# Block-sparse attention into a SwiGLU layer: the same 1,550 operations in a newly searched order

## The chip, the cores and the metric

The kernel runs on one core of a Trainium2 chip. The metric is the device time of one execution in microseconds (us). The core has five engines, each with an instruction stream of its own that it works through strictly in order: TensorE (PE in the profile, its weight loads PEld), VectorE (DVE), ScalarE (ACT), GpSimd (POOL) and SyncE (SP), which here only issues DMAs. An instruction starts when the one before it on its engine has gone ahead and the semaphores that it waits for have been raised. So the order in which each engine gets its instructions is a decision of its own, and it is the only thing that is changed here.

## The reference, cut to what matters

The first half is attention over chosen chunks of keys, the second a gated layer on its output.

```python
B, H, S, D = 4, 8, 768, 64                # chunk = 32, so 24 chunks; top_k = 6
k_min, k_max = k_chunks.min(3), k_chunks.max(3)
ub = sum(maximum(q * k_min, q * k_max), -1)          # upper bound per query and chunk
ub = where(chunk is not after the query, ub, -1e9)
top_chunks = argsort(ub)[..., -6:]
scores = where(chunk in top_chunks and key not after query, q @ k.T / 8, -1e9)
attn = softmax(scores)
x = (attn @ v).transpose(0, 2, 1, 3).reshape(3072, 512)
xn = x / sqrt(mean(x * x) + 1e-6) * rms_g
g = xn @ w_gate                           # 512 x 1536
out = (g * sigmoid(g) * (xn @ w_val)) @ w_out        # 1536 x 512
```

## The kernel before, in words

**Work and tiling.** The 3,072 tokens are cut into twelve blocks of 256 tokens, three for each of the four sequences. ORDER lists them as (sequence b, block m); position i in it is the block's number in this document: 0 to 3 are the first blocks of the four sequences, then (0,1), (1,1), (0,2), (2,1), (1,2), (3,1), (2,2) and (3,2). The eight heads go in two groups g of four heads. Each block goes through these steps, one function of the kernel each; the line numbers are those that the profile shows.

- *Loads* (`load_qk`, `load_v`, issue in `dma`, L367): q and k of a block in pieces of 64 or 128 KB, issued by SP (half of the first block's by ScalarE); v, and the weights of the second half, issued by GpSimd, which turns them into bf16 on the way.
- *Attention, one head group* (`job`): q and k are turned into rows of the head dimension by VectorE (`turn`, L632) and copied to bf16 (`half`, ScalarE L639 or GpSimd L640). VectorE takes minimum and maximum of each chunk of k (`ext0`, `ext1`, L647); `dk` is their difference (L653, GpSimd or VectorE). For blocks with m = 0, `bd` puts it into a small matrix BO (L672, either engine); for the others, VectorE writes it into BD (`KX`, L474), q is copied (`qx`, L687 or L688) and four DMAs of SP move pieces of it across partitions (`qm`, L702; by VectorE in some blocks). `relu` is max(q, 0) (L726, GpSimd or VectorE).
- *Choice of chunks* (`pick`): TensorE makes the bounds (`upper`, L518 or L536), VectorE turns them (`ubn`, L561), fills in what is barred (L568), takes the largest eight (`top`, L577), compares (`mk`, L583) and turns the mask back (`mt`, L587); `swap` makes the copy of it for the other half of the partitions (VectorE L593 or ScalarE L597 and L598).
- *Scores, exp and values* (`job`): TensorE multiplies q and k and adds the mask by two more matmuls (`scores`, L752 and L763), ScalarE takes the exp (L802), GpSimd clears the triangle above the diagonal (`tri`, L772), TensorE multiplies by v (`values`, L828) and VectorE normalises (`rden`, L843, and `norm`, L847).
- *RMS norm* (`norm`): ScalarE squares and sums (L864), GpSimd takes the root (L870, L872), the product `xs` is made by VectorE (L882, L896) or ScalarE (L898). For blocks 0 to 3, TensorE transposes it (L908) and VectorE or ScalarE writes xsT (L921, L917). For blocks 4 to 11, two transposing DMAs of SP write xsT (`across`, L888).
- *Gated layer* (`ffn`): twelve pieces of hidden units. Each has a gate and a value product (`wg`, `wv`, both L952; 8 or 16 matmuls), tanh on ScalarE (L959), a product on VectorE (`tg`, L963), and then either a copy on ScalarE (L971) and a product on GpSimd (`hh`, L974) or one product on VectorE (L967). `project` (L999) multiplies by w_out in pieces of ten and two matmuls; the result is copied out (`out`, ScalarE L1014 or VectorE L1017) and stored by SP (L1021).

**What sets the order.** Nothing is scheduled when the kernel is built. The code creates 1,550 operations, each with its dependences, its alternatives by engine (those made with `flex`) and the buffers that it takes. The list `STEPS` in class `Plan` then says in which order they are written into the engines' streams and on which engine each runs: an entry is 8 times the number of the operation plus the number of the engine (PE, ACT, DVE, POOL, SP: 0 to 4). A negative entry stands for filler: matmuls without use that keep TensorE running while it would wait (`keep_busy`, L1075); the negated number is 16 times the count (and a bit for the width: 128 or 512 columns) plus the buffer. The list `SLOTS` says which buffer of its pool each operation takes. `Plan.run` goes through the two lists. Both come from a search that is not in the kernel.

**Limits on the order.** A matmul of the gated layer needs a whole block's xsT (in blocks 0 and 1, half a block's for the first pieces). Weight loads wait for the first `dk` (`GATES`). PSUM has four buffers F of one bank for everything but the scores, which have two (S) of two banks. There are 13 buffers for hh.

Of the kernel before, what the change touches and what calls it, by code (L numbers as in the profile page):

```python
# [33 lines left out]
class Plan:  # L34
# [13 lines left out]
        139, 123, 228, 233, 131, 249, 299, 244, 260, 281, 265, 276, 99, 3, 27, 83, 50, 179, 291, 58,  # L48
        379, 385, 340, 9, 107, 348, 394, 308, 34, 403, 466, 316, 410, 356, 473, 371, 364, 450, 332,
        42, 418, 457, 324, 538, 490, 427, 115, -3296, 600, 971, 522, 609, 147, 435, 442, 482, 529,  # L50
        979, -112, 544, 498, 617, 554, 714, -82, 776, 562, 570, 506, 515, 19, 627, 785, -50, 720,
        578, 987, 586, 793, 730, 803, 1042, 995, -144, 840, 664, 594, 1049, 738, 1003, 850, -50,
        632, 746, 1114, 641, 1011, 754, 674, 649, 682, 1123, 762, 858, 769, 1058, 889, -274, 808,
        187, 91, 1098, 825, 899, 1138, 1105, 1066, 659, 1130, 817, 1075, -306, 688, 1187, 835, 1083,
        1090, 906, 1170, -51, 912, 1248, 921, 864, 698, 1146, 706, 1179, 874, -48, 1192, 1257, 1154,
        882, 1265, 1202, 929, 1162, 1362, 1275, 1210, -147, 1368, 939, 1424, 1378, 8336, 1386, 1218,
        1019, 945, 1226, 1312, 1234, 1628, 1433, 1394, 952, 1242, 8344, 1652, 1441, 962, 8353, 1644,
        1402, 1280, 1322, 1660, 8369, 8362, 8432, 1684, 1289, 1410, 8379, 1330, 1676, 1297, 8488,
        1668, 1417, 219, 1636, 1027, 8449, 8384, 8458, 1307, 1456, 8401, 1451, 1336, 1465, 8480,
        8410, 75, 1473, 1346, 1354, 1488, 8513, 1483, 1498, 8440, 8497, 1506, 1035, 1537, 8506,  # L60
        1512, 8392, 1522, 1547, 1530, 8576, 1577, 8417, 1706, 8528, 1587, 1553, 1778, 8465, 1560,
        1722, 8427, 1569, 8584, 1802, 203, 155, 1594, 1794, 8523, 8609, 1600, 8545, 1610, 8688,
        8593, 8475, 1762, 8744, 8602, 8705, 195, 1811, 2212, 1713, 1850, 8696, 8554, 8619, 2236,
        1730, 8769, 2244, 8792, 1819, 8714, 2252, 8736, 2868, 1738, 8817, 1826, 1834, 1747, 2220,
        1755, 8721, 1699, 1856, 2002, 8753, 8784, 1866, 8762, 8731, 2228, 2008, 8801, 2260, 8536,
        163, 1691, 1769, 2018, 1874, 1882, 2026, 2268, 1890, 8832, 1898, 8561, 2276, 2034, 2042,
        1785, 8840, 8571, 2050, 1906, 8849, 1912, 211, 1843, 2300, 8624, 8858, 1921, 2332, 8810,
        171, 2804, 2339, 1937, 2058, 2852, 2426, 2284, 8865, 1947, 2354, 2064, 2324, 1931, 2820,
        8632, 2370, 2073, 8827, 2292, 1976, 1952, 8656, 2316, 2089, 1962, 2442, 2308, 2083, 8641,
        1986, 1970, 2924, 2099, 2378, 2876, 8875, 1994, 2812, 2104, 2128, 2450, 2828, 8664, 2386,  # L70
        8880, 2138, 2836, 2459, 2114, 2435, 2146, 2122, 2161, 2395, 8888, 8779, 2410, 8897, 8928,
        2844, 2482, 8913, 67, 2860, 2467, 8673, 8906, 2499, 8936, 2892, 2507, 8945, 2474, 2402,
        2884, 8923, 2153, 2512, 8954, 2908, 2417, 2916, 2171, 8976, 2900, 2522, 2530, 8652, 2347,
        2538, 2185, 8684, 2546, 8961, 2178, 3540, 2554, 2361, 2946, 8971, 3476, 2192, 2561, 3580,
        9008, 2201, 3484, 2939, 2986, 3500, 3050, 3532, 3001, 3516, 2962, 2568, 2489, 3010, 8984,
        2577, 9048, 3034, 3019, 3508, 2593, 2970, 2587, 9040, 4212, 8993, 3066, 2603, 3572, 9073,
        9016, 3026, 3556, 2931, 2632, 9057, 3492, 9088, 2978, 3042, 3081, 2642, 9066, 3524, 2955,
        9025, 2656, 3092, 3058, 9105, 9083, 2608, 9096, 3100, 2665, 2650, 3564, 2618, 9136, 2626,
        2681, 2675, 3116, 9114, 9121, 9192, 3588, 2691, 3618, 9153, 4148, 9131, 9144, 3108, 9162,
        9217, 3682, 3548, 2696, 9184, 9169, 4164, 2706, 3634, 9179, 3596, 2720, 9201, 2714, 9232,  # L80
        4244, 2730, 2745, 2738, 4180, 3123, 9210, 9280, 2753, 3130, 9249, 9240, 2763, 9297, 9258,
        4196, 9288, 9265, 9227, 3722, 9004, 2777, 4236, 3136, 9306, 2769, 4188, 9275, 9313, 4204,
        3658, 2784, 4268, 3706, 9323, 9328, 4260, 2793, 3642, 4156, 4987, 3146, 5596, 3689, 4172,
        3154, 3738, 9440, 4220, 3675, 3162, 3755, 9400, 3667, 3772, 3698, 9336, 3075, 3780, 9392,
        3170, 9345, 4228, 9457, 3650, 3715, 2995, 9360, 3178, 9356, 5659, 9409, 5604, 4290, 3185,
        3788, 3730, 3627, 3745, 4252, 3603, 3192, 9425, 4354, 9368, 9418, 3201, 9448, 4306, 4860,
        9435, 4361, 1620, 4314, 9496, 9377, 3764, 4378, 3211, 3217, 9488, 4370, 4908, 9521, 4868,
# [1018 lines left out]
```

## Time and profile before

| what | us |
|---|---|
| median of three runs | 303.68 |
| lowest and highest of them | 302.05, 307.32 |
| the profiled execution | 302.84 |
| its span, first to last instruction | 301.0 |
| TensorE busy in the span (filler included) | 284.7 |
| VectorE busy | 224.1 |
| ScalarE busy | 205.9 |
| GpSimd busy | 164.2 |

The profile is of one execution. Its busy times are unions: two instructions that overlap on an engine count once. Matmuls are pipelined and their ends are modelled, so a busy TensorE can hold some idle time still. The granted clock of TensorE is 1.00 of full speed in almost all of the span (0.996 in the mean). In the rows, "x103" is a count, an arrow points from what was read to what was written, and the text after "<-" in brackets is what ended the idle time ahead of an instruction.

### The profile page before, as it was taken

To read this page: it belongs to the slowest core of one execution; us is meant where nothing else is said; L and a number is where in the kernel's file an instruction comes from. 1 tells how busy PE (TensorE), PEld (TensorE's weight loads), DVE (VectorE), ACT (ScalarE), POOL (GpSimd) and SP (SyncE) were. 2 spreads that over 40 slices of the span, in tenths; PEclk is the share of its full clock that TensorE was granted. 3 is DMA by queue.
4 is the path that set the end of the run, shared out by engine and by line. 5 is a ranking of instruction groups with operands and counts; after the bars stand their busy time and mean duration, and the time that the engine had idled before them with its cause. 6 is when DMAs were issued, how large, how long until landed. Compare 5 with 4: busy or idle time off the path is not lost.

```text
span 301.0 us, 11371 instructions
## 1 busy us (share of the span) xinstructions
PE 284.7 (95%) x4693; PEld 215.9 (72%) x4693; DVE 224.1 (74%) x649; ACT 205.9 (68%) x359; POOL 164.2 (55%) x247
## 2 busy tenths in 40 slices
PE   5989999999999889997998999999999999999994
PEld 5746887668867756886775678588688777688853
DVE  4678797988898999997899989779436455356440
ACT  3456898599869676786984698578588667544401
POOL 8576787987797668366674036168427015212330
PEclk9999999999999999999999999999999999999998
DMA  9999999868589866789664541350302004012003
GB/s 179 165 207 226 244 186 154 138 124 100 134 157 187 104 140 89 126 115 146 100 157 82 116 134 36 74 39 20 89 2 71 2 2 117 28 41 68 0 35 107
DMA packets 86387, 31.94 MB, mean 106 GB/s; under 512 B 74816, under 2 KB 81728, under 8 KB 86336
## 3 DMA queue, kind: packets, MB, share of 16 engines
q1 hardware_dynamic: 55776, 22.82, 32.1%
q0 software_dynamic: 29712, 7.87, 26.5%
q8 instruction: 37, 0.61, 0.9%
q10 hardware_dynamic: 848, 0.53, 0.7%
q14 instruction: 14, 0.11, 0.1%
HBM read 28.58 MB, written 6.29 MB: 116 GB/s over the span
## 4 chain that ended last, share of the span: by engine, by line
PE 59%; DVE 12%; DMA 12%; SPq 6%; ACT 5%; issue 3%; POOL 1%; DVEq 0%; ACTq 0%
PE F L952 30%; PE F L999 15%; DMA kraw<-in_k_dram 6%; PE S L752 5%; PE F L828 5%; SPq L367 5%; DMA rmsg<-in_moe_rms_g_dram 2%; DMA xsT<-xs 2%; PE S L763 2%; DMA out_dram<-osb 2%; DVE tg L963 1%; DVE kx L647 1%; ACT pt L802 1%; PE F L536 1%; ACT th L959 1%
## 5 line engine op out<-in xcount | busy, mean ns | idle before, releaser
L802 ACT ACTIVATE pt<-S 128x1024 bf16<-128x1024 f32 (+3 forms) x104 | 85.5, 859 | 30.6 <-PE S L763 22.5
L974 POOL TENSOR_TENSOR hh<-tg,vs 128x512 bf16<-128x512 bf16 x48 | 56.0, 1174 | 41.5 <-ACT vs L971 33.4
L952 PE MATMUL F<-xsT,wg 128*128 128x256 bf16 (+1 forms) x608 | 72.5, 267 | 2.4 <-DMA xsT<-xs 1.6
L952 PE MATMUL F<-xsT,wv 128*128 128x256 bf16 (+1 forms) x608 | 72.0, 267 | 0.2
L963 DVE SCALAR_TENSOR_TENSOR tg<-th,F 128x512 bf16<-128x512 bf16 x72 | 48.4, 677 | 29.3 <-ACT th L959 26.7
L999 PE MATMUL F<-wo,hh 128*128 128x512 bf16 (+1 forms) x300 | 68.9, 371 | 0.5 <-ACT osb L1014 0.5
L952 PEld LDWEIGHTS <-wg 128*128 128x128 bf16 x608 | 55.6, 98 | 11.5 <-issue 3.2
L952 PEld LDWEIGHTS <-wv 128*128 128x128 bf16 x608 | 55.6, 98 | 9.0 <-issue 0.4
L959 ACT ACTIVATE th<-F 128x512 bf16<-128x512 f32 x72 | 42.2, 602 | 15.5 <-PE F L952 12.1
L999 PEld LDWEIGHTS <-hh 128*128 128x128 bf16 x300 | 27.1, 98 | 26.3 <-issue 1.0
L772 POOL TENSOR_SCALAR_AFFINE_SELECT pt<-pt 128x512 bf16<-128x512 bf16 x48 | 33.2, 702 | 21.3 <-ACT pt L802 21.0
L752 PE MATMUL S<-qb,kb 32*128 32x256 bf16 (+1 forms) x800 | 33.6, 253 | 1.2 <-ACT pt L802 1.2
L971 ACT ACTIVATE vs<-F 128x512 bf16<-128x512 f32 x48 | 28.6, 602 | 7.3 <-PE F L952 6.2
L647 DVE TENSOR_REDUCE kx<-kT 128x16 f32<-128x512 f32 x48 | 31.1, 671 | 0.1
L828 PE MATMUL F<-VX,pt 128*128 128x65 bf16 x672 | 28.8, 194 | 1.6 <-DVE osb L1017 0.8
L828 PEld LDWEIGHTS <-pt 128*128 128x128 bf16 x672 | 26.0, 98 | 5.4 <-issue 1.3
L752 PEld LDWEIGHTS <-kb 32*128 32x128 bf16 x800 | 14.1, 92 | 13.4 <-issue 11.5
L367 POOL DMA_DIRECT2D VX<-in_v_dram x24 | 22.5, 939 | 0.5 <-POOL VX L416 0.3
L763 PE MATMUL S<-mto,chunkrow 32*128 32x128 bf16 (+2 forms) x384 | 20.6, 203 | 1.2 <-DVE mto L593 1.2
L763 PEld LDWEIGHTS <-chunkrow 32*128 32x128 bf16 x768 | 19.4, 93 | 2.2 <-issue 1.3
L1014 ACT ACTIVATE osb<-F 128x512 f32<-128x512 f32 (+1 forms) x17 | 9.7, 577 | 16.3 <-PE F L999 14.6
L763 PE MATMUL S<-mtd,chunkrow 32*128 32x128 bf16 (+2 forms) x384 | 20.8, 203 | 0.0
(72 smaller groups left out, 353.4 us busy)
## 6 DMA issues: line engine op xcount, KB each, us to landing
out_dram<-osb SPq DMA_DIRECT2D x23, 256.0 KB, 2.3
kraw<-in_k_dram SPq DMA_DIRECT2D x72, 64.0 KB, 3.3
qraw<-in_q_dram SPq DMA_DIRECT2D x72, 64.0 KB, 3.3
VX<-in_v_dram POOLq DMA_DIRECT2D x24, 128.0 KB, 5.0
QX<-qT SPq DMA_DIRECT2D x32, 64.0 KB, 3.3
wg<-in_moe_w_gate_dram POOLq DMA_DIRECT2D x3, 512.0 KB, 10.2
wv<-in_moe_w_val_dram POOLq DMA_DIRECT2D x3, 512.0 KB, 11.3
wo<-in_moe_w_out_dram POOLq DMA_DIRECT2D x3, 512.0 KB, 7.8
```

Of the source, the lines that this page charges most:

```text
L367: o.inst = issuer[eng].dma_start(out=dst(), in_=src)
L647: plan.op(f"ext{n}{J}", "DVE", 0.585, 0.67, lambda n=n, op=op: VE.tensor_reduce(out=at(kx)[:, g, n], in_=at(kT).rearrange("p h (j c x) -> ...
L752: TE.matmul(s[a // 2][:, a % 2, c0:c0 + q1 - q0], kbt[r, t, ks], qbt[r, t, q0:q1], start=(t == 0), stop=(t == 1 and not mask), skip_group_ ...
L763: TE.matmul(o, chunkrow[r, BLK * kg + P * e:BLK * kg + P * (e + 1)], mv, start=False, stop=(d == 1), skip_group_check=True)
L772: GE.affine_select(out=d, in_=d, compare_op=ALU.is_ge, fill=0.0, base=0, pattern=[[0, 4], [1, P]], channel_multiplier=-1)
L802: lambda pt=pt, hs=hs, c0=c0, c1=c1, x=sc[hp]: SE.activation(out=at(pt)[:, hs, c0:c1], in_=at(x)[:, :, c0:c1], func=ACT.Exp, scale=SCALE), ...
L828: TE.matmul(o[:, a, :], p_[:, a, off:off + P], vt[:, e, 4 * g + a, :], start=(kb_ == 0 and a == 0), stop=(kb_ == nkb - 1 and a == 3), skip ...
L952: TE.matmul(at(p_)[:, n * W:(n + 1) * W], w[:, g, ht * P:(ht + 1) * P], at(xT)[:, g, x0:x0 + W], start=(g == 0), stop=(g == NP - 1), skip_ ...
L959: plan.op(f"tanh{U}.{hp}", "ACT", 0.48, 0.6, lambda th=th, gp=gp: SE.activation(out=at(th), in_=at(gp), func=ACT.Tanh, scale=0.5), pri - 0 ...
L963: VE.scalar_tensor_tensor(out=at(tg), in0=at(th), scalar=1.0, in1=at(gp), op0=ALU.add, op1=ALU.mult), pri - 30, reads=[th, gp], writes=[tg ...
L974: plan.op(f"hh{U}.{hp}", "POOL", 1.11, 1.16, lambda tg=tg, vs=vs, hh=hh: GE.tensor_tensor(out=at(hh), in0=at(tg), in1=at(vs), op=ALU.mult) ...
L999: TE.matmul(at(op)[:, cs], at(key)[:, o:o + P], wo[:, ht, cs], start=(ht == 0), stop=(ht == NHT - 1), skip_group_check=True)
```

## The change: what it does, and the diff

Only `STEPS` and `SLOTS` are replaced, nearly every line of them. The operations, their code, their dependences and the number of buffers stay. The search that made the new lists counted VectorE and GpSimd as sharing a port, took the DMAs of a queue in order, and left a gap ahead of the first scores.

```diff
     STEPS = (
-        139, 123, 228, 233, 131, 249, 299, 244, 260, 281, 265, 276, 99, 3, 27, 83, 50, 179, 291, 58,
...
-        42, 418, 457, 324, 538, 490, 427, 115, -3296, 600, 971, 522, 609, 147, 435, 442, 482, 529,
+        139, 228, 249, 155, 195, 163, 27, 233, 244, 107, 50, 99, 260, 265, 34, 131, 58, 291, 281,
...
+        316, 426, 466, 364, 457, 971, 490, 115, 123, -2496, 600, 482, 539, 609, 522, 385, 434, 443,
...
     SLOTS = (
-        0, 0, 1, 0, 1, 0, 1, 0, 1, 0, 0, 0, 1, 0, 0, 1, 0, 1, 0, 0, 1, 0, 1, 1, 2, 3, 0, 0, 0, 0, 1,
...
+        0, 0, 1, 1, 0, 0, 0, 0, 1, 0, 0, 1, 0, 0, 1, 1, 0, 1, 0, 1, 2, 3, 0, 1, 0, 1, 1, 0, 0, 0, 0,
...
```

Decoded, the lists differ as follows.

| | before | after |
|---|---|---|
| operations on VectorE, ScalarE, GpSimd, SP, TensorE | 450, 319, 228, 238, 315 | 436, 316, 245, 238, 315 |
| filler, 128 columns | 103, in one run at the start | 78, in one run at the start |
| filler, 512 columns | 34, in ten places among the first 24 entries of TensorE | 27, in nine places, eight of them among its first 23 entries |
| operations on another engine | | 83 |

Among the 83: both `relu` of blocks 0 and 5 and one of blocks 1, 2, 4 and 7 from VectorE to GpSimd, both of blocks 3 and 10 and one of blocks 1 and 4 the other way; `dk` of many blocks from VectorE to GpSimd; `swap` of block 6 from VectorE to ScalarE; `xsT` of the first half of block 0 from ScalarE to VectorE; `half` and `qx` between ScalarE and GpSimd, both ways; four copies `out` from ScalarE to VectorE (blocks 0, 1 and twice 5) and four the other way (blocks 4, 6, 9 and 10).

The head, in the order of each engine (numbers in brackets are sequence, block, head group; "a" and "b" are the two halves of the first block's scores):

```
VectorE before: pat, chunkrow, turn k(0,0,0), own, turn k(0,0,1), ext0(0,0,0), turn q(0,0,0), own8, ext1(0,0,0), relu(0,0,0),
  ext1(0,0,1), turn q(0,0,1), bd1(0,0,0), ext0(0,0,1), dk(0,0,1), ubn(0,0,0), relu(0,0,1), bar, top, bd0(0,0,1), mk(0,0,0), mt(0,0,0),
  ubn(0,0,1), turn k(1,0,0), swap(0,0,0), bar, rden, top(0,0,1), turn k(1,0,1), mk(0,0,1), rden, norm, mt(0,0,1), norm, ext0(1,0,0),
  turn q(1,0,0), ext1(1,0,1), ext1(1,0,0), ext0(1,0,1), bd1(1,0,0), xs of block 0
VectorE after: pat, own, chunkrow, turn k(0,0,0), own8, ext0(0,0,0), ext1(0,0,0), turn q(0,0,0), dk(0,0,0), turn k(0,0,1),
  ext1(0,0,1), ext0(0,0,1), turn q(0,0,1), bd0(0,0,0), ubn(0,0,0), bd0(0,0,1), bar, top(0,0,0), turn q(1,0,0), mk(0,0,0), mt(0,0,0),
  turn k(1,0,0), ubn(0,0,1), rden, rden, bar, norm, norm, top(0,0,1), mk(0,0,1), ext0(1,0,0), mt(0,0,1), turn q(1,0,1), ext1(1,0,0),
  dk(1,0,0), relu(1,0,0), turn k(1,0,1), ext0(1,0,1), ext1(1,0,1), xs of block 0, dk(1,0,1), rden, bd0(1,0,0), norm, rden, norm,
  ubn(1,0,0), bd0(1,0,1), xsT of block 0
TensorE before: filler x103, scores a(0,0,0), filler x3, upper(0,0,0), filler x2, scores a(0,0,1), filler x1, upper(0,0,1), filler x4, ...
TensorE after: filler x78, scores a(0,0,0), filler x3, upper(0,0,0), upper(0,0,1), scores a(0,0,1), values(0,0,0), filler x2, ...
GpSimd before: 1 memset of ones, 1 of BO, 1 of ones, load v, memset, eps, identity, memsets, load v, load v, ..., half k(0,0,0), load v, ...
GpSimd after: 4 memsets of ones, identity, 3 memsets, load v, load v, memset, load v, memset, load v, memset, half k(0,0,0), wg load, ...
ScalarE before: 4 loads, rmsg load, early exp, half k(0,0,1), half q(0,0,0), exp, half q(0,0,1), exp, ...
ScalarE after: 4 loads, half q(0,0,0), exp, rmsg load, half q(0,0,1), exp, early exp, ...
SP before, second block: q, q, k, k, q, q, k, k          SP after: k, q, q, k, k, q, k, q
```

272 rows, old and new, of tables (SLOTS, STEPS) are left out of this document.

## The prediction

> **What bounds the kernel now.** I read the page first, then the busy time by stage, then TensorE's waits where it idles, then the head in order of time. The first line gives each engine's busy time; the next five rows cut the span into stages (length, then busy time and instructions of each engine, granted clock, DMA share, GB/s); the last row counts, in the head, only the filler matmuls of L1075.
>
> ```profile
> PE 284.7 (95%) x4693; PEld 215.9 (72%) x4693; DVE 224.1 (74%) x649; ACT 205.9 (68%) x359; POOL 164.2 (55%) x247
> ...
> 0.00:28.00 28.00, 22.41 (x390) 16.00 (x391) 18.81 (x59) 13.57 (x27) 20.09 (x47) 1.00 1.28 188
> 28.00:85.00 57.00, 56.29 (x898) 43.99 (x895) 48.92 (x143) 47.87 (x96) 45.39 (x71) 1.00 0.90 158
> 85.00:135.00 50.00, 47.24 (x892) 35.64 (x894) 47.67 (x165) 38.13 (x63) 34.60 (x50) 1.00 0.83 132
> 135.00:171.00 36.00, 33.35 (x633) 24.03 (x636) 32.35 (x90) 25.91 (x43) 19.09 (x27) 1.00 0.68 117
> 171.00:301.00 130.00, 125.39 (x1900) 96.22 (x1890) 76.36 (x196) 80.42 (x132) 45.05 (x55) 0.99 0.22 53
> ...
> 0.00:28.00 28.00, 17.36 (x137) 10.99 (x137) 1.00 1.28 188
> ```
>
> TensorE is the bound: 284.7 of 301.0 us. But 17.36 us of that is filler in the first 28 us, so until then it did only about 5 us of useful work (22.41 - 17.36). A new order adds or removes no useful matmul. It can change three things: how soon the steady work starts (28 us), the idle time after it, and the tail. From 85 to 171 us the idle time is largest: 2.76 us (50 - 47.24) and 2.65 us (36 - 33.35), 5.4 us together; the stage before loses 0.7 us. In the same stretch VectorE is busy 47.67 of 50 us, 95%, and then 32.35 of 36, 90%. It is a second bound there, and TensorE waits for what VectorE delivers late, or for what stands behind it. The next rows are TensorE's waits from 85 to 171 us (who waited for whom, us in total, times, longest).
>
> ```profile
> PE F L952 <- DMA xsT<-xs: 1.6, 1, 1.6
> PE S L752 <- ACT pt L802: 1.0, 1, 1.0
> PE F L828 <- DVE osb L1017: 0.8, 1, 0.8
> PE F L518 <- DVE qraw L726: 0.5, 1, 0.5
> ```
>
> The rows on VectorE, and the transposed xsT that comes through a VectorE product and two DMAs, are most of it.
>
> **The change part by part.** Only the lists STEPS and SLOTS differ: the same 1,550 operations, in another order on each engine, in other buffers, some on another engine that the code already allows. I decoded them by number (operation index times eight plus engine). Operations go from 450 to 436 on VectorE, from 319 to 316 on ScalarE and from 228 to 245 on GpSimd; SP keeps 238, all of them DMAs, and GpSimd its 33 DMAs. Filler goes from 103 short and 34 long matmuls to 78 and 27.
>
> *Part 1: the relief of VectorE.* These are the groups whose operations change place (busy us, mean ns of one, idle before).
>
> ```profile
> L653 DVE TENSOR_TENSOR kx<-kx 128x16 f32<-128x16 f32 x15 | 4.0, 271 | 0.1
> L726 DVE TENSOR_SCALAR qraw<-QX 128x512 f32<-128x512 f32 x5 | 3.0, 617 | 1.4 <-DMA QX<-qT 1.3
> L593 DVE STREAM_TRANSPOSE mto<-mk 64x256 bf16<-64x256 bf16 x6 | 2.6, 440 | 0.2
> L688 DVE COPY QX<-qT 128x512 f32<-128x512 f32 x2 | 0.8, 406 | 0.0
> L1017 DVE TENSOR_SCALAR osb<-F 128x512 f32<-128x512 f32 x8 | 5.5, 685 | 3.5 <-PE F L999 2.2 <-DMA out_dram<-osb 1.3
> L726 POOL TENSOR_SCALAR qraw<-QX 128x512 f32<-128x512 f32 x11 | 7.0, 640 | 15.9 <-DMA QX<-qT 13.5 <-DMA qraw<-in_q_dram 2.4
> L1014 ACT ACTIVATE osb<-F 128x512 f32<-128x512 f32 x15 | 9.0, 603 | 6.1 <-PE F L999 4.3 <-DMA out_dram<-osb 1.8
> ```
>
> Of the operations that ran between 85 and 135 us, six leave VectorE and none comes: three relus (of blocks 5 and 7) at 0.617, two differences (dk) at 0.271, and the mask swap of block 6, two transposes of 0.440: 1.85 + 0.54 + 0.88 = 3.27 us. Between 135 and 171 us two dk, one qx (0.406) and one output copy (0.685) leave, 1.63 us, and one output copy comes, 0.685: net 0.95 us. What leaves goes to GpSimd at 0.640 for a relu, or to ScalarE at 0.603 for a copy; GpSimd has 15.4 of 50 us free there, so that costs nothing as long as this room is there, and 0.64 each without it. In the first stretch VectorE has 5% slack, so I count 95% of 3.27, 3.1 us. In the second the waits are mixed with ScalarE's and the DMAs', so I count half of 90% of 0.95, 0.4 us. Sum: **3.5 us less**. The upper bound is the idle time itself, 5.4 us. The lower bound is below nothing: operations that arrive earlier can bring a loss of the same size. From 28 to 85 us VectorE gets more: two output copies, three relus and some small operations come and others go, net about 2 us, where it has 57 - 48.92 = 8.1 us free, so I count nothing; without that cover it would cost those 2 us.
>
> *Part 2: the head.* The rows are the beginning in order of time (start, length, engine, line), then two pieces of the chain that ended last.
>
> ```profile
> 3.61 8.32 PE L1075 MATMUL F<-ident 128*128 128x128 bf16 x103 [3.61 <-POOL ident masks.py:199]
> ...
> 8.18 0.71 DVE L632 STREAM_TRANSPOSE qT<-qraw 128x512 f32<-128x512 f32 x1 [1.15 <-DMA qraw<-in_q_dram]
> ...
> 8.93 1.11 ACT L639 ACTIVATE qb<-qT 128x512 bf16<-128x512 f32 x1 [1.34 <-DVE qT L632]
> ...
> 11.87 0.29 PE L752 MATMUL S<-qb,kb 32*128 32x128 bf16 x8
> ...
> 17.14 0.71 DVE L632 STREAM_TRANSPOSE kT<-kraw 128x512 f32<-128x512 f32 x1 [1.49 <-DMA kraw<-in_k_dram]
> ...
> 21.57 1.83 DVE L647 TENSOR_REDUCE kx<-kT 128x16 f32<-128x512 f32 x3
> ...
> 23.47 0.78 DVE L896 TENSOR_SCALAR xs<-xnat,ri_all 128x512 bf16<-128x512 bf16 x1
> ...
> 27.96 1.07 PE L952 MATMUL F<-xsT,wg 128*128 128x128 bf16 x16
> ```
>
> ```profile
> 3.80 5.88 DMA rmsg<-in_moe_rms_g_dram
> 9.70 7.42 DMA kraw<-in_k_dram
> ```
>
> Now the operands of the first scores are ready at 10.04 (8.93 + 1.11), but 103 fillers hold TensorE until 11.9. With the identity made after four small memsets instead of behind two loads, about 2 us sooner, and 78 fillers of 8.32/103 = 0.081 us, 6.3 us, the filler ends near 8: the first scores come at about 10, 1.8 us sooner. This gain doesn't reach the steady work, because of what is late next: the loads of the second block. In the old order VectorE waits for their last piece until 17.14 (9.70 + 7.42 is its landing) with the first head group's mask already computed. In the new order the first wait is for the q loads (turn q(1, 0, 0), VectorE's 19th operation), and queued behind it are the first block's mask (mk, mt), turn k, the second group's ub transposes, reciprocals and norms. The two sides of the landing: 15.4 us, if a load issued at 8.4 takes the median 7.0 us of the row below, and 18.6, if the four V loads, which GpSimd now issues in one run, hold the last piece by one more interval of the same size as the old wait, 1.49 us. I take 16.5: nearer 17.1, since the same sixteen loads go through the same queues, but without the rmsg load, which landed at 9.68 ahead of the last one and now comes later.
>
> ```profile
> kraw<-in_k_dram SPq DMA_DIRECT2D x10, 128.0 KB, 7.0
> ...
> L388 ACT ACT_TABLE_LOAD x1 | 1.3, 1283 | 4.2 <-DMA kraw<-in_k_dram 4.2
> L632 DVE STREAM_TRANSPOSE kT<-kraw 128x512 f32<-128x512 f32 x24 | 16.5, 695 | 2.1 <-DMA kraw<-in_k_dram 2.0
> L847 DVE TENSOR_TENSOR xnat<-F,rden 128x256 bf16<-128x256 f32 x48 | 19.7, 415 | 0.6
> ```
>
> From the landing to xs the new order has 21 operations on VectorE: four turns (0.695 each), four reductions (1.83 / 3 = 0.61), two norms (0.415) and eleven short ones (about 0.2 each, an estimate between the 0.16 of a small product, quoted under (c), and the 0.271 of a dk): 2.78 + 2.44 + 0.83 + 2.2 = 8.25 us, so xs starts at 24.7 instead of 23.47, 1.2 us later. From xs to the first FFN matmul the old order took 4.5 us (27.96 - 23.47), ScalarE's xsT and two more ub products on TensorE in it. In the new order xsT is VectorE's; xs (0.78), two norms (0.83) and six short operations (1.2) stand ahead of it, and it takes as long as a turn (0.695): 3.5 us. The first FFN matmul comes at 24.7 + 3.5 = 28.2, against 27.96: I count **0**, with -1.1 (landing at 15.4) and +2.1 (at 18.6) for the range. The 25 short and 7 long fillers that go (25 x 0.081 and 7 x 0.266, from (17.36 - 8.32)/34: 3.9 us) become idle time. The early exp that brought in the activation table moves behind ScalarE's first copy and exp. The table load then stands ahead of the first copy, and ScalarE's wait for q (1.34 us, and longer now that the cast of k leaves it) covers it; uncovered it costs the first scores up to the 1.3 us of its row, and they are not what is late.
>
> By the Trainium skill (TensorE: Matmul & The Clock Gate, Part 1) an idle window of about 3.4 us halves the clock; the granted clock is 1.00 in the head's row here, which held no such gap. Fewer fillers speak for one: by that rule alone I would estimate up to 1.7 us more.
>
> *Part 3: the queues.* In the old order the two transposing DMAs of block 5 were issued behind fifteen loads, and the first FFN matmul of that block waited 1.6 us.
>
> ```profile
> 120.11 0.58 SPq L367 DMA_DIRECT2D kraw<-in_k_dram  x1
> ...
> 129.18 0.94 SPq L367 DMA_DIRECT2D qraw<-in_q_dram  x2
> 130.22 3.43 SPq L888 DMA_TRANSPOSE xsT<-xs  x2
> ...
> 131.55 5.58 DMA xsT<-xs
> ```
>
> The first of these rows starts the fifteen, the second ends them; the last, of the chain, is the landing. In the new order seventeen loads stand between the QX copies of block 7 and these two transposes, where fifteen stood, and one piece of eight FFN matmuls less follows before block 5's first. I count no gain and no loss; 1.6 us either way is the bound. Six V loads (blocks 7, 8, 10 and 11) are issued 28 to 86 us of TensorE work later than before, which thins the queues from 30 to 130 us, where the DMA share is 0.83 to 0.90. No wait of TensorE hangs on them alone, so I count nothing; if this makes the transposes land sooner, the 1.6 us is the gain. The tail keeps its order (last FFN pieces, projection, copies, stores): 0.
>
> Sum: -3.5 + 0 + 0. The profiled execution has a span of 301.0 us in 302.84 us; it would become 297.5 in 299.3. The median of the runs shown is 303.68, 0.84 above that execution: **300.2 us**.
>
> **The rivals.** (a) *The filler's 3.9 us are a true gain of the head*: the second block's loads land near 13 and the FFN starts that much sooner: 300.2 - 3.9 = 296.3. Against it stands the landing at 17.12. (b) *The relief is given back*: VectorE is fuller from 28 to 85 us, by net 2 us, and block 5's transposes still wait; 303.68 - 3.5 + 2 + 1 = 303.2, no change. (c) *Slower, by the port.* These rows show it: a product of VectorE that takes 0.16 us alone took 0.63 while GpSimd's cast ran, and ended 0.05 us after the cast (26.06 against 26.01).
>
> ```profile
> 10.86 0.16 DVE L672 TENSOR_TENSOR BO<-kx,own 128x32 f32<-128x32 f32 x1
> ...
> 24.94 1.07 POOL L640 CAST qb<-qT 128x512 bf16<-128x512 f32 x1 [0.58 <-DVE rden L843]
> ...
> 25.43 0.63 DVE L672 TENSOR_TENSOR BO<-kx,own 128x32 f32<-128x32 f32 x1
> ```
>
> Each such meeting costs VectorE 0.47 us. With 17 more operations on GpSimd, one meeting each adds 8.0 us, if all of it falls where VectorE is the bound: 300.2 + 8.0 = 308.2. It decides from eight further meetings on (3.5 / 0.47). Against it: the same moves take 14 operations off VectorE, so that the number of pairs hardly grows. The Trainium skill (SBUF — State Buffer, on the pair of ports that VectorE and GpSimd share) has one hold it for a whole instruction while the other is fully blocked; these rows agree, 0.63 against 0.16 us. (d) *The clock*: by rows, the first 37 fillers took 3.89 us and the other 66 only 4.43, so a TensorE that has rested runs about a third slower for some 4 us. If its longest wait in the head (some 2.7 us by the working above) grows past that, 1.5 us: 301.7.
>
> ```profile
> 0.00:7.50 7.50, 3.89 (x37) 3.90 (x38) 3.41 (x6) 2.48 (x3) 6.51 (x19) 1.00 0.94 180
> ```
>
> **How the numbers follow.** The forecast has 0.45 (its own range 297 to 302), (a) 0.15, (b) 0.23, (c) 0.12, (d) 0.05. The range runs from a little under (a), 295.8, to 306.2, most of the way to (c); it leaves out most of (c) and the ends of the others. About 2% is what a measurement can tell from no change: under 297.6 or over 309.8. Faster: most of (a) and a fifth of the forecast, 0.22; slower: the upper end of (c) and what I have not seen, 0.07; the same: 0.71.
>
> **What would show it.** Part 1: VectorE's busy time between the scores of block 4 and those of block 9 falls by 3 to 4 us and TensorE's idle time there to about 2 us; wrong if VectorE's mean durations grow (the port) or if xsT is what TensorE waits for. Part 2: first scores near 10, a wait of VectorE for qraw that ends near 16.5, the first FFN matmul near 28; wrong if this matmul comes before 26 or after 30. Part 3: one wait for xsT of 1 to 2 us. The prediction falls if the FFN starts sooner by what the filler gives up, or if a new wait on GpSimd's products (L974) stops the projections.

## The result, and the profile after

The new order takes **298.99 us** in the median of four runs (298.62 to 299.62), against 303.41 for the old one beside it (302.05 to 307.32): a ratio of 0.9871, 95% interval 0.9831 to 0.9912, about 4 us or 1.3% less. The ratios here and below are of the means of the fast runs, which leaves out the old order's 307.32, over 1.5% above its fastest run. The prediction was 300.2 with a range of 295.8 to 306.2. The profiled execution has a span of 296.6 us against 301.0.

The first view is the busy time by stage of the new order, with the columns of the prediction's table.

```profile
0.00:28.00 28.00, 19.85 (x319) 13.62 (x322) 15.92 (x51) 11.47 (x23) 18.97 (x47) 0.82 1.21 189
28.00:85.00 57.00, 56.48 (x927) 44.81 (x927) 50.86 (x146) 47.29 (x97) 47.12 (x72) 1.00 0.96 159
85.00:135.00 50.00, 47.29 (x925) 36.43 (x928) 46.67 (x163) 40.66 (x68) 39.00 (x57) 1.00 0.77 133
135.00:171.00 36.00, 35.49 (x654) 26.26 (x661) 31.04 (x102) 25.16 (x41) 18.73 (x31) 1.00 0.59 116
171.00:296.60 125.60, 120.72 (x1822) 92.98 (x1828) 74.56 (x174) 79.39 (x130) 46.24 (x59) 1.00 0.28 54
```

From 85 to 171 us TensorE was idle for 5.4 us before; now it is 2.71 + 0.51 = 3.2 us. The head did not get better but worse: the granted clock there is 0.82 instead of 1.00, and 8.15 us are idle instead of 5.6. The next rows are TensorE's waits between 85 and 171 us; in the old order they held 1.6, 1.0, 0.8 and 0.5 us.

```profile
PE F L952 <- DMA xsT<-xs: 1.2, 1, 1.2
PE F L999 <- issue: 0.5, 3, 0.2
PE F L952 <- ACT osb L1014: 0.3, 1, 0.3
PE F L828 <- DVE ubn L561: 0.3, 1, 0.3
PE S L752 <- POOL qb L640: 0.3, 1, 0.3
```

Only the wait for the transposed xsT is left over 0.5 us. The row "issue" tells of a gap in the record: the profile has 300 weight loads of the projection (L999) but only 270 of its matmuls, so idle time in the new order is counted a little too high. The third view is the head in order of time, with the rows that answer to those of the prediction.

```profile
9.69 0.29 PE L752 MATMUL S<-qb,kb 32*128 32x128 bf16 x8 [1.41 <-ACT qb L639]
...
17.82 0.71 DVE L632 STREAM_TRANSPOSE qT<-qraw 128x512 f32<-128x512 f32 x1 [5.16 <-DMA qraw<-in_q_dram]
18.46 0.18 DVE L583 TENSOR_TENSOR mk<-ubn,m 128x64 bf16<-128x64 f32 x1
...
18.97 0.22 PE L763 MATMUL S<-mtd,chunkrow 32*128 32x32 bf16 x4 [3.33 <-DVE mtd L587]
...
25.17 0.34 DVE L896 TENSOR_SCALAR xs<-xnat,ri_all 128x512 bf16<-128x512 bf16 x1
...
28.55 0.68 DVE L921 TENSOR_TENSOR xsT<-F,rmsg 128x512 bf16<-128x512 bf16 x1
...
29.47 0.73 PE L952 MATMUL F<-xsT,wg 128*128 128x128 bf16 x10
```

The first scores come at 9.69 us (11.87 before). Then VectorE stands for 5.16 us, until the q of the second block has landed at 17.82. Queued behind that transpose is the first block's mask, and for it TensorE waits 3.33 us. The first FFN matmul comes 1.5 us later than before (29.47 against 27.96). So the 4.4 us of the span are the sum of a loss of 1.5 in the head, a gain of about 0.8 in the tail, and a gain of about 5.1 between. The 2.2 us of idle time that went from 85 to 171 us (5.4 less 3.2) are the part of it that the stages show; the rest is not traced to single waits. The tail: before, the last two matmuls had a gap of 0.47 us ahead of them and ended at 297.32, 3.7 us ahead of the span's end; now the last twelve run in one piece to 293.26, 3.3 us ahead of it.

```profile
296.94 0.38 PE L999 MATMUL F<-wo,hh 128*128 128x256 bf16 x2 [0.47 <-ACT osb L1014]
```

```profile
291.79 1.47 PE L999 MATMUL F<-wo,hh 128*128 128x256 bf16 x12
```

### The profile page after: what moved, and what is told of

Its sections match the earlier page's. It is cut to its first block, busy times and chain, and to the rows that moved or that the text cites. A ratio compares the mean times of both kernels' runs of the same rounds, so it can differ in the third digit from the quotient of the medians.

```text
span 296.6 us, 11267 instructions
## 1 busy us (share of the span) xinstructions
PE 279.8 (94%) x4627; PEld 214.1 (72%) x4661; DVE 219.1 (74%) x632; ACT 204.0 (69%) x356; POOL 170.1 (57%) x264
## 4 chain that ended last, share of the span: by engine, by line
PE 71%; DVE 11%; DMA 9%; SPq 3%; issue 3%; POOL 1%; ACT 1%; ACTq 0%; DVEq 0%
PE F L952 37%; PE F L999 17%; PE F L828 6%; PE S L752 6%; DMA qraw<-in_q_dram 3%; DMA wg<-in_moe_w_gate_dram 3%; SPq L367 3%; PE S L763 2%; PE F L518 2%; PE F L536 2%; DMA xsT<-xs 1%; DVE kx L647 1%; DVE m L577 1%; DMA out_dram<-osb 1%; DVE qT L632 1%
## 5 line engine op out<-in xcount | busy, mean ns | idle before, releaser
L999 PE MATMUL F<-wo,hh 128*128 128x512 bf16 (+1 forms) x270 | 65.5, 370 | 2.0 <-issue 0.8
L963 DVE SCALAR_TENSOR_TENSOR tg<-th,F 128x512 bf16<-128x512 bf16 x72 | 48.1, 678 | 18.0 <-ACT th L959 15.4
L959 ACT ACTIVATE th<-F 128x512 bf16<-128x512 f32 x72 | 42.8, 600 | 18.3 <-PE F L952 16.5
L772 POOL TENSOR_SCALAR_AFFINE_SELECT pt<-pt 128x512 bf16<-128x512 bf16 x48 | 31.7, 671 | 35.4 <-ACT pt L802 35.1
L999 PEld LDWEIGHTS <-hh 128*128 128x128 bf16 x300 | 27.5, 98 | 25.9 <-issue 0.5
L828 PEld LDWEIGHTS <-pt 128*128 128x128 bf16 x672 | 25.8, 98 | 6.3 <-POOL pt L772 2.0
L828 PE MATMUL F<-VX,pt 128*128 128x65 bf16 x672 | 27.9, 194 | 0.7 <-DVE ubn L561 0.3
L967 DVE TENSOR_TENSOR hh<-tg,F 128x512 bf16<-128x512 bf16 x24 | 16.2, 679 | 6.7 <-PE F L952 6.0
L632 DVE STREAM_TRANSPOSE qT<-qraw 128x512 f32<-128x512 f32 x24 | 16.3, 686 | 6.1 <-DMA qraw<-in_q_dram 6.1
```

Source lines behind the costliest of these rows:

```text
L772: GE.affine_select(out=d, in_=d, compare_op=ALU.is_ge, fill=0.0, base=0, pattern=[[0, 4], [1, P]], channel_multiplier=-1)
L828: TE.matmul(o[:, a, :], p_[:, a, off:off + P], vt[:, e, 4 * g + a, :], start=(kb_ == 0 and a == 0), stop=(kb_ == nkb - 1 and a == 3), skip ...
L959: plan.op(f"tanh{U}.{hp}", "ACT", 0.48, 0.6, lambda th=th, gp=gp: SE.activation(out=at(th), in_=at(gp), func=ACT.Tanh, scale=0.5), pri - 0 ...
L963: VE.scalar_tensor_tensor(out=at(tg), in0=at(th), scalar=1.0, in1=at(gp), op0=ALU.add, op1=ALU.mult), pri - 30, reads=[th, gp], writes=[tg ...
L999: TE.matmul(at(op)[:, cs], at(key)[:, o:o + P], wo[:, ht, cs], start=(ht == 0), stop=(ht == NHT - 1), skip_group_check=True)
```

## The experiments

Each kernel was timed against the old order on the same chip; ratios are to that, with 95% intervals. Edits are shown in decoded form. One theory says that the gain in the middle is VectorE's relief (Part 1), the rival that it comes from places in the order and the queues. For the head, the theories are the clock and the wait for q.

**1. The relief alone, and the new order without it.** Eleven operations of blocks 4 to 9 change engine; no place in the order changes.

```diff
 relief_undone: new order          relief_alone: old order, the same entries the other way
-GpSimd:  relu(1,1,0) relu(1,1,1) relu(2,1,1) dk(0,2,0) dk(1,1,0) dk(1,2,0) dk(3,1,1) qx(3,1,1)
-ScalarE: swap(0,2,0+1) out4.0
+VectorE: these ten
-VectorE: out5.0
+ScalarE: out5.0
```

> The new order as it is, but the ten operations of blocks 4 to 9 that it took off VectorE between 85 and 171 us go back to it, and the output copy that came (block 5) goes back to ScalarE. If their move is what shortened the middle (my step), the 3.5 us return: 302.5 us, with TensorE's lost time between 80 and 180 us up by 3 to 4 us. If the places of the operations in the order did it, the time stays within 0.8 us of 299.0.

> The old order, with only the engine of these eleven operations changed as in the new one. If their move is what counts: 303.4 - 3.5 = 299.9 us. If the places do it, 303.4 within 0.8 us; if operations that GpSimd now has to do at places searched for VectorE hold up TensorE, slower than 303.4.

Without the relief the new order takes 300.62 us, ratio 0.9953 (0.9927 to 0.9980). That is 1.6 us above the new order by the medians and 2.5 by the two ratios (0.9953 - 0.9871 = 0.0082 of 303.4), so between the two theories, which had 302.5 and 299.0 within 0.8. TensorE's idle time between 80 and 180 us did not rise by 3 to 4 us either: it is 3.62 us without the relief and 3.83 in the new order, or 2.4 there if the 1.42 us are taken off by which the projection's records fall short. The relief alone in the old order gives 302.57 against 303.15, 0.9981 (0.9942 to 1.0019): not to be told from nothing. What TensorE waits for there stands in its rows, first in the old order, then in `relief_alone`:

```profile
97.36 0.57 PE L518 MATMUL F<-QX,BD 64*32 64x128 f32 x16 [0.40 <-ACT pt L802]
98.46 0.45 PE L518 MATMUL F<-qraw,BD 64*32 64x128 f32 x16 [0.52 <-DVE qraw L726]
```

```profile
97.19 1.04 PE L952 MATMUL F<-xsT,wv 128*128 128x256 bf16 x8
99.52 0.66 PE L518 MATMUL F<-QX,BD 64*32 64x128 f32 x16 [1.29 <-DMA QX<-qT]
100.78 0.45 PE L518 MATMUL F<-qraw,BD 64*32 64x128 f32 x16 [0.60 <-POOL qraw L726]
```

The relus have moved to GpSimd, but they and the bounds read q's copy in QX, and the last piece of it lands at 99.4 us in this profile (97.2 in that of the old order; 0.8 us of the difference were there at the first FFN matmul, 28.75 against 27.96). So the two waits here grow from 0.9 to 1.9 us, while TensorE's idle time between 80 and 180 us falls from 5.75 to 4.42. At 150.5 us TensorE also waits 0.86 us for a triangle of GpSimd (0.2 in the old order); the two later kernels with the same engines do not have that wait.

**2. The copy into QX.** In the old order the last copy of block 5's group (`qm0`) stands last: between it and the two that start the group at 86.6 us SP has five loads (`gB` is one), a store and another copy, so it is issued at 91.8 and lands at 97.2 us. In the new order the last of the group lands at 94.3. The two rows below are the relus of block 5, in the old order and in the new.

```profile
97.25 1.15 DVE L726 TENSOR_SCALAR qraw<-QX 128x512 f32<-128x512 f32 x2 [1.26 <-DMA QX<-qT]
```

```profile
95.24 1.20 POOL L726 TENSOR_SCALAR qraw<-QX 128x512 f32<-128x512 f32 x2
```

So this copy was tried early in the old order, alone and with the eleven operations.

```diff
 SP in the old order (qm_early_alone; qm_early_relief has the engines of 1 as well)
 qm1(1,1), qm2(1,1)
+qm0(1,1), qm3(1,1)
 load q0220, store2.0, load q1201
-qm3(1,1)
 load q0211, load k2100, gB
-qm0(1,1)
```

> The old order with one transfer moved: the copy into QX of the half q of block 5, which SP issues behind two loads at 91.8 us and which lands at 97.2 in the profile of before, is issued right behind the other copies of its group, ahead of those loads. Theory 1 (what the new order gains between 95 and 110 us comes from this transfer's place in SP's queue more than from the ten operations that left VectorE): the relus of block 5 start near 95.5 instead of 97.3, upper(1, 1) loses its waits, TensorE's gaps at 97 to 98 us (0.4 and 0.5 us) and a part of that at 110 go, and the run takes 301.5 to 302.2 us against 303.2. Theory 2 (the place of this copy is paid for elsewhere, or VectorE is late anyway): 303.0 to 303.5, no difference, with the gaps still there.

> The same copy early and, with it, the eleven operations of blocks 4 to 9 on the engines that the new order gives them. If the two causes add, it takes the sum of their parts: 0.6 us for the engines (measured by themselves, unclear from none) and 1.0 to 1.5 for the copy, 301.0 to 301.7. If they are one cause (the relus and upper(1, 1) can use the early copy only if VectorE is free, or the free VectorE only if the copy is there), more than the sum: 299.5 to 300.7. If the rest of the order is needed (the theory that the engine orders fit only jointly): 302.3 to 303.2.

The copy alone: 302.64 against 302.94, ratio 0.9987 (0.9954 to 1.0021). With the relief: 300.24, 0.9911 (0.9883 to 0.9939), so 2.7 us less, where the two parts by themselves give 0.6 and 0.4. The excess over their sum, 1.7 us, has an uncertainty of 1.8 us by the three intervals. The early copy also brought a wait of its own, which I had not expected: the store of piece 2 now stands behind two copies, and the rows of ScalarE and TensorE, from the profile of `qm_early_alone`, show what hangs on it (0.90 us of TensorE's time with the relief).

```profile
94.37 0.60 ACT L1014 ACTIVATE osb<-F 128x512 f32<-128x512 f32 x1 [1.55 <-DMA out_dram<-osb]
```

```profile
95.02 1.03 PE L952 MATMUL F<-xsT,wg 128*128 128x256 bf16 x8 [1.29 <-ACT osb L1014]
```

Therefore the last run puts the two copies right behind that store, with the relief.

```diff
 SP in the old order, engines as in 1 (qm_behind_store)
 qm1(1,1), qm2(1,1), load q0220, store2.0
+qm0(1,1), qm3(1,1)
 load q1201
-qm3(1,1)
 load q0211, load k2100, gB
-qm0(1,1)
```

> The old order with the eleven operations on the engines of the new order, and the two last copies of block 5's QX group issued right behind the store of piece 2 instead of ahead of it (with them ahead, the store landed at 93.5 to 94.3 us instead of 90.9, ScalarE waited 1.2 to 1.6 us to write the next piece, and TensorE 0.9 to 1.3 us for ScalarE at 93 us). Theory 1 (an early copy and a VectorE relieved of the relus are needed together, and the place ahead of the store cost about 1 us of what they bring): the store lands near 91, no wait at 93 us, the relus start at 95 to 96 us, upper(1, 1) has no wait, and the run takes 298.9 to 299.8 us, against 300.2 with the copies ahead of the store. Theory 2 (the wait at 93 us was slack of the work behind it): 300.0 to 300.8, as before this edit. Theory 3 (without the rest of the order the parts bring nothing that lasts): 302 or more.

299.58 against 302.44, ratio 0.9894 (0.9845 to 0.9942): 3.2 us less, 2.2 more than the two parts by themselves, with an uncertainty of 2.1. By the ratio this can't be told from the run before it (0.9911), so the microsecond for the store's place is not shown. The profile has the steps of Theory 1, though: TensorE runs through the place where it waited.

```profile
95.90 1.21 POOL L726 TENSOR_SCALAR qraw<-QX 128x512 f32<-128x512 f32 x2
```

```profile
94.91 1.05 PE L952 MATMUL F<-xsT,wg 128*128 128x256 bf16 x8
95.79 1.04 PE L952 MATMUL F<-xsT,wv 128*128 128x256 bf16 x8
96.76 0.45 PE L518 MATMUL F<-QX,BD 64*32 64x128 f32 x16
97.16 0.45 PE L518 MATMUL F<-qraw,BD 64*32 64x128 f32 x16
```

**3. The head.** `old_head_new_rest` has the old order up to its first FFN matmul and the new order behind it.

> All operations that the old order has ahead of the first FFN matmul come in the old order, with the old engines and the old filler; all others follow in the new order. The new head starts the FFN 1.5 us later than the old one. If this delay goes through to the end: 299.0 - 1.5 = 297.5 us. If what follows the head makes up for it (loads of blocks 2 and 3, or VectorE behind them): 299.0 within 0.6.

297.25 us, ratio 0.9839 (0.9796 to 0.9883), first FFN matmul at 28.07. All but the head is worth 4.9 us (3.5 to 6.2); by the medians the new head costs the new order 1.7 us, by the ratios 1.0. Three kernels then ask what in the head costs it.

```diff
 more_filler (new order):    TensorE  + filler x12 (512 columns, buffer 2 of F) ahead of scores b(0,0,0)
 more_filler2 (new order):   TensorE  - filler x2   + filler x14, ahead of values(0,0,1)
 mask_first (new order):     VectorE  - top(0,0,0), turn q(1,0,0), mk(0,0,0), mt(0,0,0), turn k(1,0,0), ... mk(0,0,1), ext0(1,0,0), mt(0,0,1)
                                      + top(0,0,0), mk(0,0,0), mt(0,0,0), turn k(1,0,0), ... mk(0,0,1), ext0(1,0,0), mt(0,0,1), turn q(1,0,0)
                            and half q(1,0,0) moves behind swap(0,0,1)
```

> The new order with 12 more filler matmuls of 512 columns ahead of the first masked scores, where TensorE now waits from 15.6 to 19.0 us and its granted clock falls to 0.5. If the slow clock delays the FFN (rival d of the prediction): clock 1.00 throughout, first FFN matmul 1 to 1.5 us sooner, 297.5 to 298.0 us. If VectorE sets the FFN's start, the clock stays up and the time is 299.0 within 0.5.

> The new order, with 14 instead of 2 long filler matmuls ahead of the second values product, in a buffer that is free there (in the run before this, the filler wrote a buffer that VectorE still had to read, so it stood behind the wait and cost 5 us). If the slow clock delays the FFN: clock 1.00 up to 28 us, FFN 1 to 1.5 us sooner, 297.5 to 298.0 us. If VectorE sets the FFN's start: clock up, time 299.0 within 0.5.

> The new order, with the turn of the second block's q (group 0) and its cast moved behind the first block's second mask on their engines; its place ahead of the first mask is where VectorE waits 5 us for the load. If that wait and what is queued behind it delay the FFN: the first mask comes near 13.5 us instead of 18.5, TensorE has no gap of 3 us, xs starts near 23.4 instead of 25.2, the FFN 1.5 to 2 us sooner, 297.0 to 297.5 us. If the landing itself sets the FFN's start, through VectorE's work that can only be done behind it: 299.0 within 0.6.

`more_filler` did not give its theory the condition, filler during the wait: its buffer was still to be read by VectorE, behind the very wait for q, so the filler itself waited. The clock fell here too (0.50 from 14.2 to 24.4 us).

```profile
20.08 4.89 PE L1075 MATMUL F<-chunkrow,ident 128*128 128x512 bf16 x12 [4.73 <-DVE ubn L561]
```

It took 303.38 us (1.0031, 0.9993 to 1.0069), with the first FFN matmul at 34.02: a head that ends 4.6 us later than the new one costs 4.4 us. `more_filler2` took 297.73 (0.9816, 0.9769 to 0.9863); the granted clock stayed at 1.00 and the FFN came at 28.63, 0.8 us sooner. `mask_first` took 296.63 (0.9793, 0.9750 to 0.9837) with the FFN at 27.67, 1.8 us sooner, although the clock was at 0.50 from 14.4 to 21 us. By the time, 297.73 is what was expected if the slow clock delays the FFN, and 296.63 what was expected if the wait for q does, or a little less; the intervals of these two and of the new order overlap. The shift of the FFN is read from one profile each.

```profile
28.63 1.07 PE L952 MATMUL F<-xsT,wg 128*128 128x128 bf16 x16
```

```profile
12.48 0.62 DVE L583 TENSOR_TENSOR mk<-ubn,m 128x64 bf16<-128x64 f32 x1
...
27.67 1.07 PE L952 MATMUL F<-xsT,wg 128*128 128x128 bf16 x16
```

One profile cannot carry a shift of this size by itself. The new head stands unchanged in three more kernels, `sp_old_places`, `relief_undone` and `v_early`, and there the FFN starts at 28.50, 29.27 and 30.95 (the old head, in six profiles, at 27.81 to 28.75). What moves it is the end of VectorE's wait for q, at 16.62, 17.61 and 18.38 us there and at 17.82 in the new order: the FFN follows 11.9, 11.7, 12.6 and 11.65 us behind. In `more_filler2` that wait ends at 17.49, 0.3 us sooner, and the FFN follows 11.1 us behind, so the clock's price is 0.5 us or a little more. In `mask_first` VectorE waits for the second block's k first and no longer for its q, and this wait ends at 16.05; its 27.67 lies below all four starts of the unchanged head.

Both together, with turn k moved behind the second group's norms as well:

```diff
 mask_first_filler (as mask_first, and)
 VectorE: turn k(1,0,0) from behind mt(0,0,0) to ahead of mk(0,0,1)
 TensorE: filler x2 -> x6 ahead of values(0,0,1);  filler x9 -> x10 behind scores b(0,0,0)
```

> The new order with the mask of the second half of head 0 ahead of both transposes that wait for block 1's k and q, and with filler of six and ten long matmuls in place of two and nine around the masked scores, so that TensorE is never idle for over 2 us there. Theory 1 (the head's loss of 1.5 us is the clock and the wait together): the granted clock stays at 1.00 from 13 to 25 us, the first FFN matmul starts at 26.5 to 27.6 us instead of 29.5, and the run takes 295.2 to 296.6 us against 299.0. Theory 2 (only the wait behind the q load counts; with the mask first the clock is hidden, since the scaled rows xs are late next, at 23.3): FFN at 27.6 as with the mask first alone, 296.6.

298.12 us (0.9833, 0.9801 to 0.9865), FFN at 27.74, as with the mask first alone: Theory 2 for the FFN, though the time is 1.5 us over the 296.6 that went with it. The clock still fell, to 0.50 from 13.5 to 16.9 us, so Theory 1 was not given its condition, and adding filler brought nothing on top of the mask.

**4. The queues.** `sp_old_places` gives a hundred loads and QX copies of blocks 5 to 9 their old places in the new order; `v_early` does so with the six V loads.

```diff
 SP, new order (sp_old_places): q and k loads and qm copies of (1,1), (0,2), (2,1), (1,2), (3,1): behind the same TensorE operation as in the old order
 GpSimd, new order (v_early): load v210, v120, v220, v320, v321, v221: likewise
```

> The new order, but the 100 loads and QX copies that SP issues for blocks 5 to 9 come in the old order and at the old places among TensorE's operations. If the order of the queue made the middle shorter: 2 to 3.5 us of the time lost between 80 and 180 us come back, 301 to 302.5 us. If not the queue but the places on VectorE, ScalarE and TensorE: 299.0 within 0.8.

> The new order, but the six V loads that it issues 28 to 86 us later are issued at their old places. If thinner queues let the transposes and QX copies land sooner: 1 to 2 us of loss return between 80 and 180 us, 300 to 301 us. If not: 299.0 within 0.6.

The old places don't bring the old time but a worse one, 306.59 (1.0111, 1.0068 to 1.0154). One wait makes more than half of the 7.6 us to the new order: VectorE, whose new order asks here for the transpose of block 5's k, stands behind a load that the old queue issues later, and TensorE waits for the norm behind it. (The profile puts the wait down to a load of q; the row's tiles are k's, and the last load of this k lands at 80.1 us.)

```profile
80.17 0.71 DVE L632 STREAM_TRANSPOSE kT<-kraw 128x512 f32<-128x512 f32 x1 [4.89 <-DMA qraw<-in_q_dram]
```

```profile
81.46 1.87 PE L952 MATMUL F<-xsT,wv 128*128 128x256 bf16 x8 [4.43 <-DVE xnat L847]
```

So this run does not price the queues; it shows that a queue's order and VectorE's belong together. `v_early` took 300.95 (0.9924, 0.9892 to 0.9956). That is inside the 300 to 301 that was expected if thinner queues help, but its interval overlaps the new order's, and in its profile the head ended late (FFN at 30.95), which the V loads behind it can't do. TensorE is idle for 2.97 us between 80 and 180 us there, not 1 to 2 us longer than in the new order. Whether the later V loads save something stays open.

## Why the prediction was right, and where it was not

The time came out 1.2 us under the forecast; within its own range, in the case that it was given for. That it came so close is in part luck: the middle gained 5.1 us where 3.5 were counted, the tail 0.8 where nothing was, and the head lost 1.5 where nothing was. By its steps:

**Part 1, the relief, -3.5.** The place was right and the size of VectorE's relief too: between the scores of block 4 and those of block 9 VectorE's busy time fell from 94.08 to 90.01 us, and TensorE's idle time from 5.6 to 3.8 (I had said about 2). The rows are of the old order and of the new, from the first scores of block 4 to the first of block 9 in each.

```profile
90.50:193.10 102.60, 97.00 (x1875) 72.94 (x1874) 94.08 (x280) 78.19 (x128) 56.50 (x78) 1.00 0.67 117
```

```profile
90.61:188.89 98.28, 94.45 (x1796) 70.89 (x1807) 90.01 (x269) 76.18 (x124) 63.72 (x95) 1.00 0.64 120
```

But the stretch became shorter by as much, so that VectorE's share stayed at 92% (94.08 / 102.60 and 90.01 / 98.28). It also holds 79 matmuls less (1,875 and 1,796): of its 4.3 us, 2.55 are work of TensorE that is now done outside it and 1.8 are idle time. And the reason held only in half. The step that failed is "in the first stretch VectorE has 5% slack, so I count 95% of 3.27": it prices an operation that leaves by its busy time alone. Taken alone the relief is worth 0.6 us (-0.6 to 1.8) in the old order and 1.6 to 2.5 in the new. The row that told so was quoted in the prediction and not used: VectorE's L726 had 1.4 us of idle time ahead of it, 1.3 of that for the DMA into QX. The relus of block 5, which wait for a transfer, started no sooner on the other engine alone (99.53 us against 97.25). With the copies earlier the two together give 2.7 to 3.2 us, more than half of the 4.9 that all of the new order behind the head is worth. That they need each other is what the rows of these kernels speak for; by the times alone it stands at the edge of the uncertainty. The prediction named xsT as a sign against this part: it is the largest wait left, 1.2 us, but one that the old order had too, with 1.6.

**Part 3, the queues, 0.** Here those copies were missing. I compared the queue ahead of the transposes of xsT (one wait of 1.2 us is what came, as predicted), and not the places of the QX copies. How long the xsT wait is also differs between profiles of kernels that leave this part of the queue nearly the same: 1.63 before, 0.38 with the relief alone, none with the copy alone, 2.46 with both (in an execution of 303.42 us, where that kernel's median is 300.24). One profile can't carry a term of this size.

**Part 2, the head, 0.** It is a loss of 1.5 us by the two profiles, and the four profiles of the new head (28.50 to 30.95) against the six of the old one (27.81 to 28.75) bear out its sign. First scores near 10: 9.69. From q's landing to the first FFN matmul I counted 11.7 us (16.5 to 28.2), and it took 11.65 (17.82 to 29.47), but by two misses that cancel: to xs I counted 8.25 and it took 7.35 (to 25.17), and from xs I counted 3.5 and it took 4.30, with 1.18 us in it in which VectorE waited for TensorE (0.79 for values, 0.39 for bounds). So the 1.3 us between 28.2 and 29.47 are the size of the landing, 17.82 and not 16.5, inside the bounds that I gave (15.4 to 18.6). The filler's 3.9 us became idle time only in part: what is on record of it took 15.05 us instead of 17.36, as the long ones took 474 ns in the mean instead of 381, with the clock down for some of them.

**The tail, 0**: 0.8 us less.

**The rivals.** (a) is refuted: the FFN started later, not sooner. (b) would have been 303.2; the gain of the middle lasted to the end. (c), a VectorE slowed by GpSimd, is refuted at its size, 8 us, by VectorE's mean durations in the new order, 415 ns and 695 ns before (one group of the others, xs at L882, grew from 843 to 927 ns, sixteen times, 1.3 us in all):

```profile
L847 DVE TENSOR_TENSOR xnat<-F,rden 128x256 bf16<-128x256 f32 x48 | 19.7, 418 | 0.9
L632 DVE STREAM_TRANSPOSE kT<-kraw 128x512 f32<-128x512 f32 x24 | 16.5, 696 | 2.2 <-DMA kraw<-in_k_dram 2.2
```

(d) did come, on top of the forecast and by another way than written: the clock was down before the long wait began (below). The prediction's remark that the old head held no gap of that length passes over the 3.61 us ahead of its first filler, behind which the fillers ran slow, as its own row under (d) has it. Its price at the FFN is 0.5 us or a little more, by the distance from the end of the wait for q: 11.1 us with the clock up (`more_filler2`), 11.65 to 11.9 with it back at 22.4 to 23.1 us, 12.6 with it back at 25.8 (`v_early`). The order on VectorE costs as well: with the mask ahead of the wait for q, the FFN came 1.8 us sooner with the clock still down. How the loss in time divides between the two stays open, since 297.73 and 296.63 can't be told apart.

**What stays open**: the rest of the gain in the middle, 4.9 less 3.2 us, whose intervals overlap. That 'mask_first' beats the new order is likely (296.63 against 298.99), but the intervals (0.9750 to 0.9837 and 0.9831 to 0.9912) overlap at the edge; both beat the old order.

## What to carry to other kernels

Before you price an operation that moves to another engine by its busy time, read what its group waits for: an operation with DMA idle ahead of it may be worth its time only together with the transfer. In a kernel where every queue is in order, a step's price is set by what stands ahead of it on all queues that it touches; here two changes that could not be told from nothing apart took 2.7 to 3.2 us off together, and half of a fitting plan can be slower than either plan. Put work whose operands are there ahead of the one that waits for a load, and give filler a buffer that nobody behind that load has still to read. Before you read a shift of a microsecond off one profile, see how much the same stretch moves in profiles of kernels that leave it as it is: here 2.45 us.

## What the runs showed of the hardware

The granted clock fell earlier than the long gap that I had feared for it. These rows are one microsecond each of the new order (columns as above; the clock is the third number from the end).

```profile
8.00:9.00 1.00, 0.28 (x6) 0.20 (x3) 1.00 (x3) 0.45 (x1) 1.00 (x4) 1.00 1.62 188
9.00:10.00 1.00, 0.31 (x9) 0.20 (x9) 0.96 (x3) 0.64 (x1) 1.00 (x4) 1.00 1.61 173
...
12.00:13.00 1.00, 0.60 (x32) 0.59 (x32) 0.63 (x6) 0.60 (x3) 0.83 (x2) 0.94 1.39 191
13.00:14.00 1.00, 0.79 (x18) 0.48 (x14) 0.00 (x0) 0.51 (x2) 0.23 (x1) 0.50 1.33 188
...
22.00:23.00 1.00, 1.00 (x4) 0.45 (x3) 0.97 (x3) 0.93 (x4) 0.87 (x2) 0.50 1.25 207
23.00:24.00 1.00, 1.00 (x16) 0.44 (x16) 0.97 (x4) 0.33 (x2) 0.51 (x2) 0.94 1.23 206
```

It was down at about 12.9 us (0.94 is 0.88 us at 1.00 and the rest at 0.50), when the longest gap since the start of the filler was the 1.41 us ahead of the first scores, from 8.28 us, followed by 3 us of TensorE at 60 to 73%; the gap of 3.33 us began at 15.64. It came back at about 23.1, some 4 us after TensorE had begun to run without gaps. In the profiles with the new head's filler up to there the clock fell 4 to 5.5 us after the first run of filler had ended: the gap ahead of the first scores began at 7.92 and lasted 2.27 us, and the clock fell at 12.1 (`v_early`); 8.28, 1.41 and 12.9 (the new order); 8.56, 1.78 and 13.4 (`mask_first_filler`); 8.99, 0.49 and 14.4 (`mask_first`); `sp_old_places`, `relief_undone` and `more_filler` lie between. Only in `more_filler2` (8.85 and 0.95), where fourteen long fillers in a row follow at 13.5, it did not fall. The stretches at half clock lasted 3.41 us (`mask_first_filler`, 13.45 to 16.86), 6.83 (`mask_first`), 10.24 (the new order, 12.88 to 23.12, and the three just named) and 13.66 (`v_early`): 1, 2, 3 and 4 times 3.41. So here the clock came back only in steps of that length, and how soon after the gaps ended is partly a matter of where the step fell. The Trainium skill (TensorE: Matmul & The Clock Gate, Part 1) has the clock halve after an idle window of about 3.4 us. The half (0.50) agrees, and so does the length as that of a step; a gap of that length was not needed, a broken-up stretch did it, and here the measurement decides.
